# Two feed-forward networks behind pooled attention on one core: attention half-steps re-spaced, low terms moved to VectorE, output products lagging two tiles, weight loads re-queued

## The chip, the core and the metric

The kernel runs on one core of a Trainium2 chip. The metric is the device time of one execution in microseconds. Engines are named as in the profile: PE (TensorE matmuls) and PEld (its weight loads), DVE (VectorE), ACT (ScalarE), POOL (GpSimd), SP (SyncE, which only issues transfers here). Transfers are issued by SP (hardware queue q1) or by POOL (software queue q0).

## The reference, cut to what matters

```python
# attention: q, k, v are (8, 8, 576, 64); k and v are averaged over groups of 8 keys -> 72 keys
scores = (q @ k_p.T) / 8;  attn = exp(scores - max);  attn /= attn.sum() + 1e-9
x = (attn @ v_p) as (4608, 512)
# first network, d_ff = 2048
h = x @ w_in;  x = (s * relu(h)**2 + b) @ w_out
# second network, d_ff = 1536
out = (sigmoid(x @ w_gate) * (x @ w_val)) @ w_out2
```

Weights come as float64. Every large product is made of three float32r products, hi·lo + hi·hi + lo·hi, so each operand is split in a high part (an ACT copy) and a low part (a subtraction).

## The kernel before, in words

**Stage 1 (attention and first network).** The 4608 tokens are 9 blocks of 512. For each block `j` and each of `M1` = 16 slices `m` of d_ff there is one step `i`: `emit_h(i)` (L201, 12 matmuls into `hps`), ReLU, square, scale and bias, `split_g(i)` (L223, makes `gh` on ACT and `gl` on DVE), and `emit_x(i - 2)` (L233, 12 matmuls into four `acc` tiles). Weight slices arrive on SP (`load_wi`, L119) into three buffers. The second network's weights are prepared meanwhile by `prep_w2` (L170): float64 words come in by SP, ACT and DVE convert them (`convert`, L73, `cv` and `raw` tiles), POOL subtracts, SP stores them to DRAM (`w7d`, `wo2d`).

Attention is cut in 18 units of 256 tokens with two halves `t` of 128. A table of positions, two per step (L460 to L487), says where each part of a unit stands; position 2i is ahead of `emit_h(i)`, 2i+1 ahead of `emit_x(i - 2)`. The parts are `scores` (L371: matmuls into `sps`, maximum and subtraction on DVE, exponential on ACT), `norm` (L393: sum and reciprocal on DVE, then POOL makes `pl`, the probabilities of the last 8 keys, and `pm`, those of the first 64), `left` (L408: high copies of `pl` on ACT, low terms on POOL at L414, into `lt`), `turn` (L417: PE transposes `pm` into `tm` and `lt` into `tl`; ACT and DVE copy them out as `t`), and `values` (L439: matmuls into `pv`, split into `xh` and `xl`, which `emit_h` of the next block reads). `sps`, `tm`, `tl` and `pv` share the two buffers of the pool `ps_c`. The pooled keys and values of the next batch are summed on POOL (`kv`, `kbd`, `s` tiles).

From step 16 on PE's order is the program's own (L609). Before that, and on all other engines throughout, a scheduler sets each engine's order from its own model of the times; each engine then works its list strictly in order.

**Stage 2 (second network).** Four pairs of token blocks (`pairs`, L556) are multiplied with seven products in place of eight, then one plain block. In a pair, for each of `M2` = 12 slices: `first_half` (L680, 24 matmuls), `second_half` (L695, 18 matmuls), and `emit_o(p, m, 0)` (L705, 12 matmuls) for the first block of the pair. The gated values of the second block are kept in SBUF, and after the 12 slices come 12 `emit_o(p, m, 1)`: the **kept stretch**. `fetch_w7` (L644) loads 1792 KB for a slice into one of two buffers, from SP. `fetch_wo` (L651) loads 512 KB of `w_out2` into one of three buffers, from POOL. `gen_x` (L568) makes the next pair's operands in the kept stretch from `load`s (L562, POOL, into the six `cv` buffers, which the output copies `eo` use too). The buffers of stage 2 lie where stage 1's weights were, and a load waits for the last reader of the tile it replaces.

```python
for m in range(M2):                    # L739
    fetch_wo((p, 0, m))
    half = first_half(p, m)
    if m:
        emit_o(p, m - 1, 0)
    second_half(p, m, *half)
    fetch_w7(p, m + 2)
emit_o(p, M2 - 1, 0)
```

Of the kernel before, what the change touches and what calls it, by code (L numbers as in the profile page):

```python
# [8 lines left out]
F32 = mybir.dt.float32  # L9
# [3 lines left out]
ALU = mybir.AluOpType  # L13
# [6 lines left out]
def pooled_attention_two_ffn(ctx, tc, q, k, v, v_left, w_in, w_out, s_in, b_in, w_gate, w_val, w_out2, out):  # L20
# [8 lines left out]
    nc = tc.nc  # L29
# [8 lines left out]
    M2 = w_gate.shape[0]  # L38
# [20 lines left out]
    NBLK = len(blocks)  # L59
    w1d = [dram.tile([128, 2, 512], F32, name=f"w1d{m}") for m in range(M1)]  # L60
    w7d = [dram.tile([128, 2, 8 * 256], F32, name=f"w7d{m}") for m in range(M2)]
    wo2d = [dram.tile([128, 2, 512], F32, name=f"wo2d{m}") for m in range(M2)]
    x2d = [dram.tile([128, KD, n], F32, name=f"x2d{j}") for j, (_, n) in enumerate(blocks)]
# [169 lines left out]
    def emit_x(i):  # L233
        j, m = steps[i]
        n = blocks[j][1]
        if m == 0:
            acc[j] = [ps_a.tile([128, 512], F32, tag="a", name="acc")[:, :n] for _ in range(KD)]
        gh, gl = g_t.pop(i)
        hi, lo = wo[m]
        for d in range(KD):  # L240
            f = slice(d * 128, (d + 1) * 128)
            nc.tensor.matmul(out=acc[j][d], lhsT=hi[:, f], rhs=gl, start=m == 0, stop=False)  # L242
            nc.tensor.matmul(out=acc[j][d], lhsT=hi[:, f], rhs=gh, start=False, stop=False)  # L243
            nc.tensor.matmul(out=acc[j][d], lhsT=lo[:, f], rhs=gh, start=False, stop=m == M1 - 1)  # L244
        if m == M1 - 1:
            for d, a in enumerate(acc.pop(j)):
                eo = cvp.tile([128, 512], F32, tag="cv", name="eo")[:, :n]
                if d % 2:
                    nc.vector.tensor_copy(out=eo, in_=a)
                else:  # L250
                    nc.scalar.activation(out=eo, in_=a, func=ACTF.Copy)
                nc.sync.dma_start(out=x2d[j][:, d, :], in_=eo)


    mask = const.tile([128, 3], F32, name="mask")
# [152 lines left out]
    def left(u, t):  # L408
        pm, pl = e_t[u, t]
        lt = at2.tile([128, H, 4, 8], F32R, tag="lt", name="lt")  # L410
        for sl in (0, 2):
            nc.scalar.activation(out=lt[:, :, sl], in_=pl, func=ACTF.Copy)
        for sl in (1, 3):
            nc.gpsimd.tensor_tensor(out=lt[:, :, sl], in0=pl, in1=lt[:, :, sl - 1].bitcast(F32), op=ALU.subtract)  # L414
        e_t[u, t] = pm, lt

    def turn(u, t, part):  # L417
# [44 lines left out]
    def at(pos, fn, *args):  # L462
        events.setdefault(pos, []).append((fn, args))

    for b in range(1, B):
        p = 16 * (b * S // UNIT - 2)
# [9 lines left out]
    for u in range(2, NU):  # L476
        p = 16 * (u - 2) + (2 if u == 2 else 0)
        for t, o in ((0, 0), (1, 4)):
            at(p + o, scores, u, t, 0)
            at(p + o, scores, u, t, 1)  # L480
            at(p + o + 2, norm, u, t)
            at(p + o + 3, left, u, t)
            at(p + o + 6, turn, u, t, 0)
            at(p + o + 6, turn, u, t, 1)
        at(p + 7, load_q, u + 2)
        at(p + 14, values, u, 0)
        at(p + 14, values, u, 1)  # L487

    def probs(u, t):
        scores(u, t, 0, True)  # L490
# [6 lines left out]
    with tc.manual_schedule():  # L497
# [24 lines left out]
        norm(0, 0, True)  # L522
        pool_v_pe(0, "v")
        left(0, 0)
        probs(1, 0)
        norm(0, 1, True)
# [18 lines left out]
    if True:  # L545
# [61 lines left out]
        for i in range(NS):  # L607
            if i == M1:
                pe_order.enter_context(tc.manual_schedule(engines={mybir.EngineType.PE}))  # L609
            store_later()  # L610
            for fn, args in events.pop(2 * i, []):
                fn(*args)
            load_wi(i + 3)
            emit_h(i)
            x, r = divmod(i - 18, 9)
            if i >= 18 and x < M2:
                prep_w2(x, r)
            split_wi(i + 2)
            split_g(i)
            split_wo(i + 1)  # L620
            load_wo(i + 2)
            for fn, args in events.pop(2 * i + 1, []):
                fn(*args)
            if i >= LAG:
                emit_x(i - LAG)
            last = i - (NS - M1)
            if last == 0:
                assert not any(p < 2 * NS for p in events), events
                at_stack.close()
                xop = ctx.enter_context(tc.tile_pool(name="xop", bufs=1, side="right", reuse_waits="tile"))  # L630
            if last in (3, 7):
                gen_x(0, last // 7)


        for i in range(NS - LAG, NS):
            emit_x(i)
        w1_stack.close()
        w7p = ctx.enter_context(tc.tile_pool(name="w7p", bufs=2, reuse_waits="tile"))
        wo2p = ctx.enter_context(tc.tile_pool(name="wo2p", bufs=3, reuse_waits="tile"))
        g2p = ctx.enter_context(tc.tile_pool(name="g2p", bufs=1, reuse_waits="tile"))  # L640
        wk = ctx.enter_context(tc.tile_pool(name="wk", bufs=10, reuse_waits="tile"))
        w7, wo2, g2 = {}, {}, {}

        def fetch_w7(p, m):  # L644
            p, m = p + m // M2, m % M2
            if p < len(pairs):
                a, n = (0, 5) if p == NPAIR else (1, 7)
                w7[p, m] = w7p.tile([128, 2, 7, 2, 128], F32R, tag="w7", name="w7")[:, :, :n]
                nc.sync.dma_start(out=w7[p, m].rearrange("p a b c d -> p a (b c d)").bitcast(F32), in_=w7d[m][:, :, 256 * a:256 * (a + n)])

        def fetch_wo(key):  # L651
            wo2[key] = wo2p.tile([128, 2, 512], F32R, tag="wo2", name="wo2")
            nc.gpsimd.dma_start(out=wo2[key].bitcast(F32), in_=wo2d[key[2]])  # L653

        def product(ps, p, m, x, first, right=None):
            w, r, n = w7[p, m], xo[p][x if right is None else right], pairs[p][1]
# [23 lines left out]
        def first_half(p, m):  # L680
            n = pairs[p][1]
            b0, b1 = (ps_b.tile([128, 512], F32, tag="b", name="pb")[:, :n] for _ in range(2))
            b2, b3 = (ps_c.tile([128, 512], F32, tag="c", name="pc")[:, :n] for _ in range(2))
            product(b0, p, m, 0, True)
            p1 = wk.tile([128, 512], F32, tag="wk", name="wk")[:, :n]
            nc.scalar.activation(out=p1, in_=b0, func=ACTF.Copy)
            product(b1, p, m, 4, True)
            u2 = add2(b1, p1, n)
            product(b2, p, m, 5, True)
            u3 = add2(b2, u2, n)  # L690
            product(b3, p, m, 2, True)
            c22 = add2(b3, u3, n)
            return b0, b2, b3, u2, c22

        def second_half(p, m, b0, b2, b3, u2, c22):  # L695
            n = pairs[p][1]
            product(b0, p, m, 1, False)
            product(b2, p, m, 3, False)
            c21 = add2(b2, u2, n)
            gated(p, m, 0, b0, c21)  # L700
            product(b3, p, m, 6, False)
            c12 = add2(b3, u2, n)
            gated(p, m, 1, c12, c22)

        def emit_o(p, m, t):  # L705
            t0, n = pairs[p]
            if m == 0:
                acc[p, t] = [ps_a.tile([128, 512], F32, tag="a", name="acc") for _ in range(n // 128)]
            gh, gl = g2.pop((p, m, t))
            w = wo2.pop((p, t, m))  # L710
            hi, lo = w[:, 0], w[:, 1]
            for x, a in enumerate(acc[p, t]):
                f = slice(128 * x, 128 * x + 128)
                nc.tensor.matmul(out=a, lhsT=gl[:, f], rhs=hi, start=m == 0, stop=False)  # L714
                nc.tensor.matmul(out=a, lhsT=gh[:, f], rhs=hi, start=False, stop=False)  # L715
                nc.tensor.matmul(out=a, lhsT=gh[:, f], rhs=lo, start=False, stop=m == M2 - 1)  # L716
                if m == M2 - 1:
                    eo = cvp.tile([128, 512], F32, tag="cv", name="eo")
                    if x % 2:
                        nc.vector.tensor_copy(out=eo, in_=a)  # L720
                    else:
                        nc.scalar.activation(out=eo, in_=a, func=ACTF.Copy)
                    r0 = t0 + t * n + 128 * x
                    nc.sync.dma_start(out=out[r0:r0 + 128, :], in_=eo)
# [11 lines left out]
        fetch_w7(0, 0)  # L736
        fetch_w7(0, 1)
        for p in range(NPAIR):
            for m in range(M2):  # L739
                fetch_wo((p, 0, m))  # L740
                half = first_half(p, m)
                if m:
                    emit_o(p, m - 1, 0)
                second_half(p, m, *half)
                fetch_w7(p, m + 2)
            emit_o(p, M2 - 1, 0)
            for m in range(3):
                fetch_wo((p, 1, m))
            gen_x(p + 1, 0)
            gen_x(p + 1, 1)  # L750
            for m in range(M2):
                emit_o(p, m, 1)
                if m + 3 < M2:
                    fetch_wo((p, 1, m + 3))
        if NB % 2:
            for m in range(M2):
                fetch_wo((NPAIR, 0, m))
# [47 lines left out]
```

## Time and profile before

| | |
|---|---|
| median of 3 runs | 1847.71 us (1847.41 to 1849.23) |
| the profiled execution's own time | 1847.31 us |
| its span, first to last instruction | 1845.5 us |
| PE busy | 1752.0 us (95%), 8032 matmuls |
| PEld, DVE, ACT, POOL busy | 1449.9, 933.5, 696.5, 454.2 us |
| mean granted clock of PE | 0.98 of full speed |
| transfers | 364 MB, mean 197 GB/s |

A matmul of 128x512 is drawn about 0.39 us long, while the next one starts 0.23 us after it: matmuls are pipelined. So PE's idle time as the profile gives it (until the next start, from the drawn end) is about 0.16 us short of what a stall costs. "PEclk" is the clock that PE was granted, 1.0 for 2.4 GHz and 0.5 for 1.2 GHz.

### The profile page before, as it was taken

The numbers are of one execution on the slowest core, as the hardware profiler recorded it, in microseconds if no ns is written. First come the engines' busy times: TensorE is split into PE (matmuls) and PEld (weight loads), VectorE is DVE, ScalarE is ACT, GpSimd is POOL, SyncE is SP. The second block draws the span as 40 slices with busy tenths as digits, with TensorE's granted clock in tenths as the row PEclk, the third lists the DMA queues.
The fourth block names the chain that finished last, engine by engine and source line by source line (L and its number), as shares of the span: only waits on it lengthen the run. The fifth ranks groups of instructions, "written<-read, shape, count | busy, mean of one in ns | idle before, by whom it ended". The sixth has DMA issues, their size and how long they took to land.

```text
span 1845.5 us, 21515 instructions
## 1 busy us (share of the span) xinstructions
PE 1752.0 (95%) x8032; PEld 1449.9 (79%) x8032; DVE 933.5 (51%) x1455; ACT 696.5 (38%) x1222; POOL 454.2 (25%) x571
## 2 busy tenths in 40 slices
PE   5888898998999999999998999999999999999999
PEld 4677787887888878788886887788778877887787
DVE  7997745655355555544442445445544554454111
ACT  2666544454454545454442222222222222222111
POOL 6855615425154433322000000200020002000100
PEclk7899999999999999999999999999999999999999
DMA  6775745746375655534433556655575557555764
GB/s 235 267 237 200 262 137 190 251 151 221 99 248 184 224 187 187 201 131 154 139 128 130 197 194 204 242 201 197 192 255 201 196 193 251 194 200 174 248 227 166
DMA packets 103353, 364.22 MB, mean 197 GB/s; under 512 B 10193, under 2 KB 17361, under 8 KB 103249
## 3 DMA queue, kind: packets, MB, share of 16 engines
q1 hardware_dynamic: 84816, 296.78, 46.6%
q0 software_dynamic: 18432, 66.07, 10.6%
q8 instruction: 64, 1.05, 0.2%
q14 instruction: 41, 0.33, 0.1%
HBM read 304.09 MB, written 58.72 MB: 197 GB/s over the span
## 4 chain that ended last, share of the span: by engine, by line
PE 48%; issue 28%; DMA 6%; POOL 5%; DVE 2%; ACT 0%; POOLq 0%; SPq 0%; DVEq 0%; ACTq 0%
PE hps L211 5%; PE hps L213 5%; PE hps L212 5%; PE acc L244 5%; PE acc L242 5%; PE acc L243 5%; PE acc L714 2%; PE acc L716 2%; PE acc L715 2%; DMA wo<-wo2d 2%; PE pc L658 2%; PE pc L660 2%; PE pc L659 2%; DMA raw<-in 2%; PE pb L658 1%
## 5 line engine op out<-in xcount | busy, mean ns | idle before, releaser
L664 DVE TENSOR_TENSOR wk<-pc,wk 128x512 f32<-128x512 f32 x192 | 132.4, 690 | 251.6 <-PE pc L660 251.6
L653 POOL DMA_DIRECT2D wo<-wo2d x108 | 57.1, 529 | 817.6 <-PE acc L716 760.9
L211 PE MATMUL hps<-xl,wi 128*128 128x512 f32 (+1 forms) x584 | 237.6, 407 | 10.6 <-ACT wi L55 6.5
L56 DVE TENSOR_TENSOR gl<-g,gh 128x512 fp32r<-128x512 f32 x204 | 159.6, 782 | 166.4 <-ACT gh L55 161.5
L213 PE MATMUL hps<-xh,wi 128*128 128x512 f32 (+1 forms) x584 | 230.7, 395 | 0.8 <-POOL wi L56 0.8
L212 PE MATMUL hps<-xh,wi 128*128 128x512 f32 (+1 forms) x584 | 229.7, 393 | 0.0
L242 PE MATMUL acc<-gl,woh 128*128 128x512 f32 x576 | 225.8, 392 | 3.9 <-DVE gl L56 3.8
L243 PE MATMUL acc<-gh,woh 128*128 128x512 f32 x576 | 224.5, 390 | 0.0
L244 PE MATMUL acc<-gh,wol 128*128 128x512 f32 x576 | 224.3, 390 | 0.0
L55 ACT ACTIVATE gh<-g 128x512 fp32r<-128x512 f32 x204 | 128.3, 629 | 144.1 <-DVE g L676 141.2
L219 DVE TENSOR_TENSOR g<-g 128x512 f32<-128x512 f32 x128 | 100.2, 783 | 158.5 <-ACT g L215 158.4
L675 ACT ACTIVATE g<-pb 128x512 f32<-128x512 f32 x60 | 35.8, 597 | 359.8 <-PE pb L660 359.8
L659 PE MATMUL pc<-xo,w 128*128 128x512 f32 x432 | 168.1, 389 | 0.0
L658 PE MATMUL pc<-xo,w 128*128 128x512 f32 x432 | 168.1, 389 | 0.0
L660 PE MATMUL pc<-xo,w 128*128 128x512 f32 x432 | 168.1, 389 | 0.0
L220 ACT ACTIVATE g<-g,b_sb,s_sb 128x512 f32<-128x512 f32 x144 | 117.2, 814 | 104.3 <-DVE g L219 103.2
L215 ACT ACTIVATE g<-hps 128x512 f32<-128x512 f32 x144 | 85.2, 592 | 153.0 <-PE hps L213 152.2
L658 PE MATMUL pb<-xo,w 128*128 128x512 f32 x336 | 131.6, 392 | 8.3 <-DMA w<-w7d 8.3
L211 PEld LDWEIGHTS hps<-xl,wi 128*128 128x128 f32 x584 | 112.8, 193 | 33.1 <-ACT wi L55 7.7
L213 PEld LDWEIGHTS hps<-xh,wi 128*128 128x128 f32 x584 | 112.5, 193 | 24.8 <-POOL wi L56 1.0
L659 PE MATMUL pb<-xo,w 128*128 128x512 f32 x336 | 131.2, 391 | 0.0
L660 PE MATMUL pb<-xo,w 128*128 128x512 f32 x336 | 131.2, 390 | 0.0
(109 smaller groups left out, 3342.9 us busy)
## 6 DMA issues: line engine op xcount, KB each, us to landing
w<-w7d SPq DMA_DIRECT2D x48, 1792.0 KB, 7.7
wi<-w1d SPq DMA_DIRECT2D x128, 512.0 KB, 3.7
wo<-wo2d POOLq DMA_DIRECT2D x108, 512.0 KB, 3.8
raw<-in SPq DMA_DIRECT2D x68, 512.0 KB, 4.8
w7d<-raw SPq DMA_DIRECT2D x36, 512.0 KB, 3.7
w<-w7d SPq DMA_DIRECT2D x12, 1280.0 KB, 6.5
kv<-in SPq DMA_DIRECT2D x24, 512.0 KB, 5.4
kv<-in SPq DMA_DIRECT2D x16, 576.0 KB, 4.1
```

The lines of the kernel that those rows point to most:

```text
L55: nc.scalar.activation(out=hi, in_=src, func=ACTF.Copy)
L56: eng.tensor_tensor(out=lo, in0=src, in1=hi.bitcast(F32), op=ALU.subtract)
L211: nc.tensor.matmul(out=ps[:, f], lhsT=hi[:, kk], rhs=c[:, kk, f], start=kk == 0, stop=False)
L212: nc.tensor.matmul(out=ps[:, f], lhsT=hi[:, kk], rhs=a[:, kk, f], start=False, stop=False)
L213: nc.tensor.matmul(out=ps[:, f], lhsT=lo[:, kk], rhs=a[:, kk, f], start=False, stop=kk == KD - 1)
L242: nc.tensor.matmul(out=acc[j][d], lhsT=hi[:, f], rhs=gl, start=m == 0, stop=False)
L243: nc.tensor.matmul(out=acc[j][d], lhsT=hi[:, f], rhs=gh, start=False, stop=False)
L244: nc.tensor.matmul(out=acc[j][d], lhsT=lo[:, f], rhs=gh, start=False, stop=m == M1 - 1)
L658: nc.tensor.matmul(out=ps, lhsT=w[:, 0, x, kk], rhs=r[:, 1, kk, :n], start=first and kk == 0, stop=False, skip_group_check=True)
L659: nc.tensor.matmul(out=ps, lhsT=w[:, 0, x, kk], rhs=r[:, 0, kk, :n], start=False, stop=False, skip_group_check=True)
L660: nc.tensor.matmul(out=ps, lhsT=w[:, 1, x, kk], rhs=r[:, 0, kk, :n], start=False, stop=kk == 1, skip_group_check=True)
L664: nc.vector.tensor_tensor(out=o, in0=ps, in1=b_, op=ALU.add)
```

## The change

- `values(u, 0)` and `values(u, 1)` stand at positions p + 12 and p + 13 in place of both at p + 14. The positions of `turn` are written in another way and stay the same numbers (p + 6 and p + 10).
- `left`'s low terms are computed by DVE, not POOL.
- The four stores of the last block (`x2d` of block 8) are issued by POOL, not SP.
- `fetch_wo` is issued by SP, not POOL, and has four buffers, not three.
- `emit_o(p, m, 0)` comes two slices late, not one; the last two come together after the last `second_half`.
- Of the kept stretch's twelve `w_out2` tiles two are asked for in the last slice and two among the last output products; the fetch of the next pair's second `w7` tile is written after `emit_o(p, 4, 1)`.

```diff
@@ emit_x
-                nc.sync.dma_start(out=x2d[j][:, d, :], in_=eo)
+                (nc.gpsimd if j == NBLK - 1 else nc.sync).dma_start(out=x2d[j][:, d, :], in_=eo)
@@ left
         for sl in (1, 3):
-            nc.gpsimd.tensor_tensor(out=lt[:, :, sl], in0=pl, in1=lt[:, :, sl - 1].bitcast(F32), op=ALU.subtract)
+            nc.vector.tensor_tensor(out=lt[:, :, sl], in0=pl, in1=lt[:, :, sl - 1].bitcast(F32), op=ALU.subtract)
@@ the table of positions
-            at(p + o + 6, turn, u, t, 0)
-            at(p + o + 6, turn, u, t, 1)
+            if t == 0:
+                at(p + 6, turn, u, 0, 0)
+                at(p + 6, turn, u, 0, 1)
+        at(p + 10, turn, u, 1, 0)
+        at(p + 10, turn, u, 1, 1)
         at(p + 7, load_q, u + 2)
-        at(p + 14, values, u, 0)
-        at(p + 14, values, u, 1)
+        at(p + 12, values, u, 0)
+        at(p + 13, values, u, 1)
@@ stage 2
-        wo2p = ctx.enter_context(tc.tile_pool(name="wo2p", bufs=3, reuse_waits="tile"))
+        wo2p = ctx.enter_context(tc.tile_pool(name="wo2p", bufs=4, reuse_waits="tile"))
@@ fetch_wo
-            nc.gpsimd.dma_start(out=wo2[key].bitcast(F32), in_=wo2d[key[2]])
+            nc.sync.dma_start(out=wo2[key].bitcast(F32), in_=wo2d[key[2]])
@@ the loop over pairs
+            kept = [(p, 1, m) for m in range(M2)]
             for m in range(M2):
                 fetch_wo((p, 0, m))
                 half = first_half(p, m)
-                if m:
-                    emit_o(p, m - 1, 0)
+                if m >= 2:
+                    emit_o(p, m - 2, 0)
+                if m == M2 - 1:
+                    fetch_wo(kept.pop(0))
+                    fetch_wo(kept.pop(0))
                 second_half(p, m, *half)
-                fetch_w7(p, m + 2)
-            emit_o(p, M2 - 1, 0)
-            for m in range(3):
-                fetch_wo((p, 1, m))
+                if m < M2 - 1:
+                    fetch_w7(p, m + 2)
+            for m in (M2 - 2, M2 - 1):
+                emit_o(p, m, 0)
+                fetch_wo(kept.pop(0))
             gen_x(p + 1, 0)
             gen_x(p + 1, 1)
             for m in range(M2):
                 emit_o(p, m, 1)
-                if m + 3 < M2:
-                    fetch_wo((p, 1, m + 3))
+                if kept:
+                    fetch_wo(kept.pop(0))
+                if m == 4:
+                    fetch_w7(p, M2 + 1)
```

SP's list where stage 1 ends, before (`wi` is stage 1's weights, `x2d_126` the last block's result, `w` a slice of `w7d`):

```order
L127 DMA wi<-w1d_93 128x1024
L252 DMA x2d_126<-eo 128x512 x2
L649 DMA w_8633<-w7d_94 128x2x1792
L252 DMA x2d_126<-eo 128x512 x2
L649 DMA w_8635<-w7d_95 128x2x1792
L649 DMA w_8711<-w7d_96 128x2x1792
```

and now:

```order
L127 DMA wi<-w1d_93 128x1024
L652 DMA w_8633<-w7d_94 128x2x1792
L652 DMA w_8635<-w7d_95 128x2x1792
L656 DMA wo_8637<-wo2d_106 128x1024
L656 DMA wo_8713<-wo2d_107 128x1024
L656 DMA wo_8789<-wo2d_108 128x1024
L656 DMA wo_8881<-wo2d_109 128x1024
L652 DMA w_8711<-w7d_96 128x2x1792
```

The first two `w` loads no longer stand behind stores of the last block, which are on POOL's list now.

SP's list now where the first pair's last slice ends and its kept stretch begins (`w7d_105` is that slice's weights, `w7d_94` and `w7d_95` the next pair's first two; `wo` from `wo2d_106` on are the kept tiles):

```order
L652 DMA w_9495<-w7d_105 128x2x1792
L656 DMA wo_9635<-wo2d_106 128x1024
L652 DMA w_9583<-w7d_94 128x2x1792
L656 DMA wo_9637<-wo2d_107 128x1024
L652 DMA w_9850<-w7d_95 128x2x1792
L656 DMA wo_9687<-wo2d_108 128x1024
L727 DMA out<-eo 128x512 x2
L656 DMA wo_9713<-wo2d_109 128x1024
L727 DMA out<-eo 128x512 x2
L656 DMA wo_9792<-wo2d_110 128x1024
```

Two kept tiles moved ahead of the next pair's second `w` load. That load, which the program writes after the fifth kept product, stands ahead of the third kept tile all the same.

DVE's list where the second half of unit 6 is normalised, before (the reciprocal ends `norm`; `gl` and `g` belong to the steps, `t` to `turn`):

```order
L398 RECIPROCAL sm<-sm 128x8
L56 TENSOR_TENSOR gl<-g,gh 128x512
L219 TENSOR_TENSOR g<-g 128x512
L56 TENSOR_TENSOR gl<-g,gh 128x512
L219 TENSOR_TENSOR g<-g 128x512
```

and now:

```order
L398 RECIPROCAL sm<-sm 128x8
L56 TENSOR_TENSOR gl<-g,gh 128x512
L219 TENSOR_TENSOR g<-g 128x512
L56 TENSOR_TENSOR gl<-g,gh 128x512
L414 TENSOR_TENSOR lt<-pl,lt 128x8x8 x2
L219 TENSOR_TENSOR g<-g 128x512
```

The low terms, which stood on POOL behind sums of the next batch, now stand on DVE between two of the steps' operations.

## Rows read from the trace of the kernel before

**Rows 1.** Windows by stage (us; busy of each engine with counts, clock, DMA, GB/s)

```profile
0.00:166.00 166.00, 124.25 (x588) 101.63 (x589) 146.89 (x219) 94.61 (x181) 111.43 (x116) 0.89 0.70 241
```

**Rows 2.** Waits of PE (us in total, times, longest)

```profile
PE tl L436 <- POOL lt L414: 11.7, 4, 4.3
PE acc L714 <- DMA wo<-wo2d: 9.4, 7, 2.8
PE pb L658 <- DMA w<-w7d: 8.3, 1, 8.3
...
PE sps L378 <- DVE xl L56: 7.3, 4, 3.7
...
PE acc L714 <- DVE gl L56: 6.4, 4, 1.6
```

**Rows 3.** Timeline of SP and POOL where stage 2's first loads are issued

```profile
957.11 11.20 SPq L127 DMA_DIRECT2D wi<-w1d  x3
...
992.20 0.58 SPq L649 DMA_DIRECT2D w<-w7d  x1
992.83 1.09 SPq L252 DMA_DIRECT2D x2d<-eo  x2
993.96 0.57 SPq L649 DMA_DIRECT2D w<-w7d  x1
...
954.66 0.53 POOL L653 DMA_DIRECT2D wo<-wo2d  x1 [29.83 <-PE acc L244]
```

**Rows 4.** Landing times by tile: `x2d` of 992.8 to 993.6, `w` of 992 to 995

```profile
DMA to landing us min/median/max: 9.7/9.8/9.8
...
DMA to landing us min/median/max: 8.4/11.4/14.4
```

**Rows 5.** Timeline of PE: the end of the first pair's last slice

```profile
1146.02 0.39 PE L659 MATMUL pc<-xo,w 128*128 128x512 f32 x1
1146.25 0.39 PE L660 MATMUL pc<-xo,w 128*128 128x512 f32 x1
...
1148.25 0.50 PE L714 MATMUL acc<-wo,gl 128*128 128x512 f32 x1 [1.61 <-DVE gl L56]
```

**Rows 6.** Windows behind stalls (PE busy third, clock third from last)

```profile
226.00:236.00 10.00, 6.29 (x19) 5.03 (x19) 7.60 (x12) 3.20 (x6) 3.60 (x4) 0.51 0.86 282
318.20:321.20 3.00, 3.00 (x9) 2.42 (x9) 0.40 (x1) 1.95 (x4) 2.26 (x4) 0.51 0.77 225
425.00:430.40 5.40, 5.40 (x15) 4.25 (x14) 0.40 (x1) 1.32 (x3) 5.09 (x8) 0.50 0.72 218
1000.70:1003.80 3.10, 3.10 (x7) 2.47 (x8) 0.00 (x0) 0.14 (x1) 0.00 (x0) 0.50 1.05 398
1160.80:1164.20 3.40, 3.40 (x10) 2.62 (x9) 1.99 (x3) 0.96 (x2) 0.57 (x2) 0.51 0.78 296
```

**Rows 7.** Transfers (page, part 6: count, KB each, median us from issue to landing)

```profile
w<-w7d SPq DMA_DIRECT2D x48, 1792.0 KB, 7.7
```

**Rows 8.** Timeline of POOL, ACT and PE around unit 6's second half

```profile
317.29 0.59 POOL L414 TENSOR_TENSOR lt<-pl,lt 128x64 fp32r<-128x64 f32 x2
...
311.91 0.40 ACT L412 ACTIVATE lt<-pl 128x64 fp32r<-128x64 f32 x2 [0.90 <-POOL pl L405]
...
317.93 0.69 PE L436 MATMUL tl<-ident,lt 128*128 128x128 f32 x2 [4.34 <-POOL lt L414]
```

**Rows 9.** Timeline of DVE: beside a busy POOL, and idle

```profile
303.52 1.61 DVE L56 TENSOR_TENSOR gl<-g,gh 128x512 fp32r<-128x512 f32 x1
...
312.83 1.35 DVE L219 TENSOR_TENSOR g<-g 128x512 f32<-128x512 f32 x1 [3.60 <-ACT g L215]
...
213.26 0.43 DVE L81 TENSOR_SCALAR raw<-raw 128x512 int32<-128x512 int32 x1 [4.37 <-DMA raw<-in]
```

**Rows 10.** Timeline of PE and DVE: the longest way from `turn` to `t`

```profile
524.83 0.60 PE L430 MATMUL tm<-ident,pm 128*128 128x128 f32 x4
...
529.68 0.69 DVE L56 TENSOR_TENSOR t<-tm,t 128x512 fp32r<-128x512 f32 x1
```

## The prediction

> **What bounds the kernel now.** PE does. I read the windows by stage first, then PE's own waits, then the timelines at each long wait, then the clock behind them. In the opening 166 us PE is busy 124 and DVE 147 us [rows 1]: DVE leads there. After it PE is nearly always busy, and what can be won is the short list of stalls in PE's waits [rows 2]. The change aims at five of its entries. Each stall costs about 0.16 us more than its idle time, because a matmul is drawn 0.39 us long while the next starts 0.23 us later [rows 5]. Behind some stalls the clock stands at half, 1.2 GHz in place of 2.4 [rows 6]; of PE's busy time at half clock, half is lost.
>
> **Start of stage 2: -10.0 us.** PE waits 8.3 us for the first `w` load [rows 2]. SP issues it only at 992.2, behind two stores of the last block, although the last `wi` loads are out by 968 (957.1 + 11.2) [rows 3]. In SP's new list the stores are gone and `w` follows `wi`. Its buffer lies where early slices of the first network's output weights were: a `w_out2` load, placed above it, had its buffer free at 954.7 [rows 3]. So `w` can go out at about 968 and, at 7.7 us [rows 7], land at 976, before PE's last product of stage 1 at 992. The stall of 8.3 + 0.16 goes, and with it half of 3.1 us at half clock [rows 6]: 8.5 + 1.5 = 10.0. The stores on POOL cost nothing: their readers come in the plain block, 700 us on. If the buffer were free only with the last product, nothing would be won.
>
> **Output products two slices late: -7.1 us.** After a pair's last slice PE waits 1.61 us for `gl` (1148.25, the slice's last matmul having started at 1146.25) [rows 5], once in each of four pairs, 6.4 in all [rows 2]. Now `emit_o` of slice 10 stands in between: 12 matmuls by 0.23 = 2.7 us, more than the 2.0 us from the end of the slice until `gl` is there. 4 x (1.61 + 0.16) = 7.1. What is hidden costs again if DVE is more than 0.7 us later. Slice 1 runs without output products now, as slice 0 does already without a stall.
>
> **The kept stretch: -13.9 + 2.0 us.** PE waits seven times, 9.4 us, for kept tiles [rows 2]: 9.4 + 7 x 0.16 = 10.5, and two windows of 3.4 us at half clock follow (one shown [rows 6]) at 1.7 each: 13.9. Two tiles are now loaded in the last slice. The third is what is late next: SP's list has it behind the next pair's second `w` load. From the end of the slice, T: `w` is issued at once and lands at T + 7.9. How queued transfers of SP follow each other shows at 994: the last `x2d` store lands at 993.5 + 9.8 = 1003.3, the `w` behind it at 994.0 + 14.4 = 1008.4 [rows 3, 4], 5.1 us for 1792 KB, so 1.46 us per 512 KB. The third tile lands at T + 9.4 and is needed at T + 4 x 2.72 = 10.9. Two output stores (1.5) and the fourth tile (1.5): 12.3, needed 13.6. Two stores and the fifth tile: 15.2, needed 16.3; but two or three loads of `gen_x` (0.73 each) may come between, and it can be 0.4 to 1.1 us late. I take 0.5 per pair, 2.0 in all; between 0 and the whole 13.9. The other kept tiles have three products of lead.
>
> The Trainium skill (DMA: Bandwidth & Descriptors, Queues, rings and completion order) says that the DMA engines take turns between queues and work one queue in its ring's order. By it the move to SP gives up a turn: on POOL's queue the third tile would share the engines with `w` at once, on SP's it stands behind it. By it alone the kept stalls would stay: that is rival K. The trace agrees on the order within SP's queue [rows 4].
>
> **Low terms on DVE and values earlier: -14.0 us.** At 318 and 425 PE waits 4.34 and about as long for `tl`: ACT has both copies at 312.3, but POOL makes the low terms only at 317.3 to 317.9, behind sums for the next batch [rows 8]. DVE idles 3.60 us until 312.83 there [rows 9] and would do two operations (0.3 each, as on POOL [rows 8]) by 313. So 2 x 4.35 = 8.7 goes, and half of 3.0 and of 5.4 us at half clock [rows 6]: 4.2. Earlier `values` free the `ps_c` buffers earlier; of the 7.3 us that `scores` wait for `xl` [rows 2], two short ones (some 1.1 with the 0.16 each) go. The rest is two stalls at 222 to 231. There DVE waits 4.37 us for weights until 213.26 [rows 9] and then has a backlog ahead of `xl`; in its new list the same conversions stand ahead of `xl`, so I let it stay, 0 of up to 9.7 (6.6 idle, half of 6.29 us busy at half clock [rows 6]). `values` now come one step after `turn`: 24 matmuls by 0.227 and the transposes' own 0.6 [rows 10], some 6.0 us. The longest that `t` took after step 16 is 5.5 (524.83 to 530.37) [rows 10]: no new wait.
>
> **The opening: +1.0 us.** Units 0 to 3 put 16 low terms on DVE, 16 x 0.3 = 4.8 us where DVE leads; PE in return loses its `lt` waits there, 11.7 - 8.7 = 3.0 [rows 2]. Net 1.8 if all of DVE's time counts; I take 1.0. The lower end is -3.0. The upper end: beside a busy POOL DVE took 1.61 us for what takes it 0.69 elsewhere, 0.9 more [rows 9, 10]; on all 16 that is 19. The scheduler's order of PE in this part moves too, which no row prices; I put it within the same bounds.
>
> **Sum**, against the profiled execution's own 1847.3 us (0.4 under the median of the runs): 1847.3 - 10.0 - 7.1 - 13.9 + 2.0 - 14.0 + 1.0 = **1805 us**.
>
> **Rivals.**
> K, the kept stretch stays bound by transfers: `w` in front of the third tile keeps the stalls, moved from the POOL queue to SP's. For it: the deferral of `w` is undone in SP's list. Against it: the margins of 1.1 to 1.5 us above. 1805 + 11.9 = 1817.
> O, DVE pays in the opening: the low terms run beside POOL's sums, half of them 0.9 us longer, and nothing of `lt`'s wait comes back: 4.8 + 7.2 = 12.0 in place of 1.0, 1816. The Trainium skill (SBUF — State Buffer, Terms) says that DVE and GpSimd share a port pair as an exclusive lock, held for a whole instruction. By it a low term on DVE waits out a POOL operation, which speaks against this edit; the trace agrees in direction (1.61 against 0.69).
> S, the stall at 222 goes as well, since `values` are in hand earlier than the conversions: 1805 - 9.7 = 1795.
> M, the change of the stores does nothing: `w` waits for its memory, not for SP. 1815. The free buffer at 954.7 speaks against it.
> Q, slower: `wo` loads on SP wait for PE and hold up the `w` loads behind them. A `w` load is issued at a slice's end and needed one slice later, 54 x 0.227 = 12.2 us; it takes 7.7, so 4.5 us late is free, and what is more costs PE that much in each of some 46 slices. At 1 us over, 1805 + 46 = 1851. Against it: the `wo` load in front waits for `emit_o` in the same slice, 18 matmuls or 4.1 us before the `w` buffer comes free.
>
> **How the numbers follow.** Forecast 0.45, K 0.15, O 0.13, S 0.12, M 0.05, Q 0.04, and two of K, O and M together (1826 or so) 0.06. From 1793, just under S, to 1821, over K and O with some error in each, leaves out Q, the pairs and some tails, under 2 in 10. A difference of 0.2%, 3.7 us, is about what a measurement can tell from no change. All but Q are faster by more; Q's milder forms reach no change: 0.94 faster, 0.02 the same, 0.04 slower.
>
> **What would show it.** PE's wait for `w` at the start of stage 2 gone, with the load issued near 968; no wait for `gl` at L714's new line; at most some 2 us of waits for `wo`; no wait of `tl` for `lt` near 313 and 420, and no half clock behind them; PE reaching 166 us's work within a few us of before. It is wrong if kept tiles still stall PE 2 us and more a pair, if `w` is issued after 990, if PE waits for `lt` on DVE, or if a new wait for `w` shows inside the slices.

## The result and the profile after

The changed kernel takes **1814.93 us** (median of 4 runs, 1814.27 to 1816.36), against 1847.56 for the kernel before in runs beside it: a ratio of 0.9824, 95% interval 0.9807 to 0.9841. The forecast was 1805, the range 1793 to 1821. So it is faster by 1.8%, 33 us in place of the 42 that were forecast. The profiled execution took 1814.27 us, its span is 1812.5. Of all the executions below, one (1957.66 us, in e4, at a clock of 0.84 in place of 0.98) belongs to a slower state and is left out.

Where the gain lies is read from the starts of PE's matmuls, one at each border of a stretch (us; the forecast's terms sorted the same way):

| stretch | before | after | difference | forecast |
|---|---|---|---|---|
| up to the first matmul of step 16 | 172.90 | 175.73 | +2.8 | +1.0 |
| from there to stage 1's last matmul | 819.15 | 816.45 | -2.7 | -14.0 |
| from there to stage 2's first | 8.64 | 0.22 | -8.4 | -8.5 |
| stage 2, to the end of the span | 844.9 | 820.1 | -24.8 | -20.5 |

Stage 2 did a little more than was forecast. Stage 1 as a whole gained nothing, where 13 us were forecast. One trace tells a gain of a few us there from none only roughly: the changed kernel and e5 to e8 below have the same list on each engine in stage 1, and their five traces take 804.9 to 811.8 us from the first matmul of step 16 to that of step 143. The opening's row, answering [rows 1] (columns as there):

```profile
0.00:166.00 166.00, 119.50 (x575) 98.03 (x576) 148.65 (x233) 90.70 (x174) 100.91 (x100) 0.89 0.70 240
```

PE's waits in the changed kernel (total, times, longest), answering [rows 2]:

```profile
PE tm L430 <- DVE e L386: 11.4, 4, 4.0
PE acc L242 <- DVE gl L56: 11.0, 6, 5.6
PE sps L378 <- DVE xl L56: 8.3, 4, 3.3
...
PE tl L436 <- DVE lt L414: 5.7, 7, 1.7
```

The waits for `w`, for `wo` and for stage 2's `gl` (8.3, 9.4 and 6.4 us before) are gone: from 985 us to the end the view names no wait at all. At the head now stands a wait of `turn`'s transposes (`tm`) for DVE's `e`, which was 4.6 us before.

**Start of stage 2.** SP's timeline, answering [rows 3], and PE's where stage 1 ends:

```profile
957.24 11.20 SPq L127 DMA_DIRECT2D wi<-w1d  x3
968.49 1.49 SPq L652 DMA_DIRECT2D w<-w7d  x2
970.02 2.94 SPq L656 DMA_DIRECT2D wo<-wo2d  x4
```

```profile
992.18 0.39 PE L244 MATMUL acc<-gh,wol 128*128 128x512 f32 x1
992.40 0.39 PE L661 MATMUL pb<-xo,w 128*128 128x512 f32 x1
```

The first `w` is issued at 968.49, 24 us earlier, and PE goes from one stage to the next without a gap.

**The kept stretch.** PE's last slice of the first pair ends where the output products of slice 10 begin, answering [rows 5], and SP issues around it:

```profile
1133.62 0.39 PE L663 MATMUL pc<-xo,w 128*128 128x512 f32 x1
1133.85 0.39 PE L717 MATMUL acc<-wo,gl 128*128 128x512 f32 x1
```

```profile
1134.04 0.52 SPq L652 DMA_DIRECT2D w<-w7d  x1
1136.76 0.33 SPq L656 DMA_DIRECT2D wo<-wo2d  x1
1138.07 1.11 SPq L727 DMA_DIRECT2D out<-eo  x2
1139.48 0.33 SPq L656 DMA_DIRECT2D wo<-wo2d  x1
```

With T = 1133.85, the third kept tile goes out at T + 2.9 (behind `w`, and when its buffer is free) and, by the transfer view's 6.9 us from issue to landing, is there at T + 9.8; it is needed at T + 10.9. The fourth (7.4 us) is there at T + 13.0 and needed at T + 13.6. Both margins were forecast within 0.7 us, and neither is overdrawn.

**Clock.** In stage 2 there is no stretch at half clock before the last 2 us; before there were three. In stage 1 four are left after step 16, each behind a wait, answering [rows 6] (PE busy third, clock third from last); one of them:

```profile
561.80:565.20 3.40, 3.40 (x9) 2.63 (x9) 2.28 (x6) 2.17 (x7) 3.20 (x5) 0.50 0.96 321
```

**Stage 1.** The wait for `lt` around unit 6's second half, 4.34 us in [rows 8], is down to 0.27, and so is its twin of unit 8. PE and DVE there:

```profile
311.18 0.66 PE L430 MATMUL tm<-ident,pm 128*128 128x128 f32 x4 [0.78 <-POOL pm L405]
312.10 0.41 PE L436 MATMUL tl<-ident,lt 128*128 128x128 f32 x2 [0.27 <-DVE lt L414]
```

```profile
310.44 1.52 DVE L414 TENSOR_TENSOR lt<-pl,lt 128x64 fp32r<-128x64 f32 x2 [2.96 <-ACT lt L412]
```

What took the gain away stands at unit 7, 11 and 13, first halves. PE, DVE and POOL at unit 11:

```profile
556.29 0.39 PE L244 MATMUL acc<-gh,wol 128*128 128x512 f32 x1
560.70 0.63 PE L430 MATMUL tm<-ident,pm 128*128 128x128 f32 x4 [4.02 <-DVE e L386]
```

```profile
555.78 1.99 DVE L414 TENSOR_TENSOR lt<-pl,lt 128x64 fp32r<-128x64 f32 x2 [0.48 <-ACT lt L412]
557.69 1.77 DVE L56 TENSOR_TENSOR gl<-g,gh 128x512 fp32r<-128x512 f32 x1
559.38 0.81 DVE L385 TENSOR_REDUCE mx<-sps 128x4 f32<-128x288 f32 x2
560.11 0.81 DVE L386 TENSOR_TENSOR e<-sps,mx 128x288 f32<-128x288 f32 x2
```

```profile
554.72 0.74 POOL L405 TENSOR_TENSOR pl<-e,sm 128x64 f32<-128x64 f32 x1
...
556.43 3.61 POOL L284 TENSOR_TENSOR kv<-kv 128x512 f32<-128x512 f32 x3
```

`turn(u, 0)` at p + 6 needs the `ps_c` buffers that the second half's `scores` (p + 4) fill, and DVE empties them with `mx` and `e`. In DVE's list those stand behind a step's `gl`, and now `gl` stands behind two low terms. Beside POOL's sums the low terms take 1.99 us and `gl` 1.77; `gl` alone takes 0.69. PE waits 4.02 us and then runs 3.4 us at half clock (561.80, above). The low terms themselves are the smaller part here: ACT has `gh` ready at 557.26, so they hold up `gl` by 0.4 us, and e1 below, without any of them on DVE, still waits 2.80 us at this place. `pl` is late too, behind POOL's sums, and ACT's copies of it stand ahead of the step's own work on ACT.

### The profile page after: what moved, and what is told of

Read it like the earlier page. It is cut to its first block, busy times and chain, and to the rows that moved or that the text cites. A ratio compares the mean times of both kernels' runs of the same rounds, so it can differ in the third digit from the quotient of the medians.

```text
span 1812.5 us, 21425 instructions
## 1 busy us (share of the span) xinstructions
PE 1741.0 (96%) x8032; PEld 1445.5 (80%) x8032; DVE 965.1 (53%) x1527; ACT 693.9 (38%) x1222; POOL 367.1 (20%) x395
## 4 chain that ended last, share of the span: by engine, by line
PE 73%; DVE 9%; DMA 8%; POOL 5%; issue 3%; ACT 2%; SPq 0%; POOLq 0%; DVEq 0%; ACTq 0%
PE acc L719 5%; PE pc L663 5%; PE pc L661 5%; PE acc L717 5%; PE pc L662 5%; PE acc L718 5%; PE hps L211 4%; PE hps L213 4%; PE hps L212 4%; PE acc L242 4%; PE pb L661 4%; PE pb L663 4%; PE pb L662 4%; PE acc L243 4%; PE acc L244 4%; DMA raw<-in 4%
## 5 line engine op out<-in xcount | busy, mean ns | idle before, releaser
L568 POOL DMA_DIRECT2D cv<-x2d x36 | 19.5, 542 | 724.5 <-DMA out<-eo 338.3
L242 PEld LDWEIGHTS acc<-gl,woh 128*128 128x128 f32 x576 | 108.8, 189 | 35.9 <-DVE gl L56 13.9
L661 PE MATMUL pb<-xo,w 128*128 128x512 f32 x336 | 130.7, 389 | 0.0
L662 PE MATMUL pb<-xo,w 128*128 128x512 f32 x336 | 130.7, 389 | 0.0
```

What stands on the lines that cost most here:

```text
L661: nc.tensor.matmul(out=ps, lhsT=w[:, 0, x, kk], rhs=r[:, 1, kk, :n], start=first and kk == 0, stop=False, skip_group_check=True)
L662: nc.tensor.matmul(out=ps, lhsT=w[:, 0, x, kk], rhs=r[:, 0, kk, :n], start=False, stop=False, skip_group_check=True)
```

## The experiments

All times are medians. A stretch between two matmuls is read from one trace of each kernel. The kernel before, run beside each group, took 1846.64 (the first four), 1844.54 (the next four), 1847.84 (three) and 1845.64 us (the last).

### Which edit of stage 1 gave the gain back

Theory V: `values`, one step earlier, put work in front of `e`. Theory D: the low terms on DVE do.

**e1**, low terms back on POOL:

```diff
-            nc.vector.tensor_tensor(out=lt[:, :, sl], ...
+            nc.gpsimd.tensor_tensor(out=lt[:, :, sl], ...
```

> The changed kernel with the low terms back on POOL; values early, stage 2 as changed. Theory D (DVE's list: low terms that wait for POOL's late pl, or run beside POOL, hold up the subtractions of the scores behind them): PE's waits of tm for e fall from 11.4 us back to about the 4.6 of before, with the half clock behind them (some 11 us together), and its waits of tl for lt come back near 313 and 420 (8.7 + 4.2 us): time about 1815 to 1818. Theory V (the early values put the splits of pv ahead of the steps' work on DVE and so make e late): the waits for e stay at 11 us and the tl waits come on top: about 1828.

**e2**, `values` back at p + 14:

```diff
-        at(p + 12, values, u, 0)
-        at(p + 13, values, u, 1)
+        at(p + 14, values, u, 0)
+        at(p + 14, values, u, 1)
```

> The changed kernel with both values back at p + 14; low terms on DVE, stage 2 as changed. Theory D: the waits of tm for e near 355, 560 and 667 stay (11 us in all), scores wait for xl some 1 to 3 us more: 1815 to 1819. Theory V: the waits for e fall to 4.6 us or less with their half clocks: about 1804.

**e3**, both diffs above together, so that only the edits at the end of stage 1 and in stage 2 are left:

> Low terms on POOL and values at p + 14, stage 1 as in the kernel before; only the stores of the last block and stage 2 changed. If the sum by stages of the two traces holds (stage 1 of the changed kernel took what it took before, all of the gain is from the last product of stage 1 on), this is the kernel before less 33 us: 1814.5, the same as the whole change. If stage 1's edits are worth their 14 us and something else ate them, it is about 1828.

**e4**, POOL's `pl` on DVE as well, so that DVE's low terms wait for POOL no longer:

```diff
-            nc.gpsimd.tensor_tensor(out=o, in0=e[:, :, j], ...
+            (nc.vector if o is pl else nc.gpsimd).tensor_tensor(out=o, in0=e[:, :, j], ...
```

> The changed kernel with pl, the probabilities of the last 8 keys, computed by DVE too, so that DVE's low terms no longer wait for POOL (pm stays on POOL). Theory D: the waits of tm for e near 355 and 560 go (7 us, and half of the 3.4 us half clock behind each), the tl waits stay away: about 1804 to 1808. Theory V: nothing changes there, 1815 plus the 36 operations more on DVE, 1815 to 1818.

Measured, with the table's stretches by the first matmuls of steps 16 and 143:

| kernel | median us (ratio to before, 95%) | step 16 at | 16 to 143 |
|---|---|---|---|
| before | | 172.9 | 808.5 |
| changed | 1814.93 (0.9807 to 0.9841) | 175.7 | 805.8 |
| e1 low on POOL | 1811.78 (0.9782 to 0.9822) | 171.9 | 806.0 |
| e2 values at 14 | 1819.02 (0.9839; 0.9818 to 0.9861) | 176.9 | 808.0 |
| e3 both | 1811.88 (0.9782 to 0.9822) | 174.3 | 805.3 |
| e4 `pl` on DVE | 1814.82 (0.9782 to 0.9844) | 177.3 | 804.5 |

The two edits of stage 1 together do not bring the 13 us: e3 without them is at 1811.88, 3 us below the changed kernel, which the intervals do not tell apart. V falls, since e2 keeps the waits for `e` (11.7 us in 4) and is not at V's 1804. D holds for the opening: with low terms on DVE step 16 begins at 174.6 to 177.5 in all nine kernels of this study that have them there, wholly or in first halves (mean 176.3); with low terms on POOL at 170.8 to 174.3 in five (mean 172.4): 3.9 us. Its form "DVE waits for POOL's `pl`" falls with e4: without that wait `tm` still waits 9.7 us for `e` from 166 us on, against 11.4. From step 16 to 143 D is not the whole: in e1, without any low term on DVE, the waits for `e` are 7.8 us (with 2.8 that the view puts down to `kv`, see e10) and those for `lt` are back, and it takes the same 806 us. Early `values` do not settle it either: e1 is 8.2 us ahead of e3 at step 24 (224.5 against 232.8; 2.5 of them were there at step 16), with the wait at 222 down to 1.7 us, and of these 1.7 are left at step 112. The waits of e1 from 166 to 985 us are others than those of the changed kernel:

```profile
PE tl L436 <- POOL lt L414: 8.7, 2, 4.3
PE tm L430 <- DVE e L386: 5.0, 2, 4.0
PE tm L430 <- POOL kv L284: 2.8, 1, 2.8
```

### The edits of stage 2, one undone at a time

Stage 1, which these edits leave alone, differs by up to 7 us between these traces, and the kernel before took 3 us less beside these four than beside the changed kernel. So each is also measured in its profile from the first matmul of step 143 to the end: 831.0 us in the changed kernel, and the same within 0.02 us in the eight others here whose stage 2 is as changed.

**e5**, the last block's stores back on SP:

```diff
-                (nc.gpsimd if j == NBLK - 1 else nc.sync).dma_start(out=x2d[j][:, d, :], in_=eo)
+                nc.sync.dma_start(out=x2d[j][:, d, :], in_=eo)
```

> The changed kernel with one part undone: the last block's four stores are issued by SP again. Theory (SP's list held up the load): the first w load is issued near 983 to 991, behind the first two stores, PE waits some 8 us for it at the start of stage 2 and stands at half clock behind that; +8.5 to +10.0 us, 1823 to 1825. Rival M (the load waits for its memory, and the change's gain there comes from elsewhere): the load goes out at the same time as in the changed kernel, no new wait, 1815 within 2.

1825.18 us, +10.3; from step 143 on +10.8. SP and PE:

```profile
998.95 1.10 SPq L252 DMA_DIRECT2D x2d<-eo  x2
1000.09 0.58 SPq L652 DMA_DIRECT2D w<-w7d  x1
```

```profile
1008.47 0.80 PE L661 MATMUL pb<-xo,w 128*128 128x512 f32 x1 [8.14 <-DMA w<-w7d]
```

`w` waits behind the stores again. The forecast's term of 10.0 is right; rival M falls.

**e6**, output products one slice late:

```diff
-                if m >= 2:
-                    emit_o(p, m - 2, 0)
+                if m:
+                    emit_o(p, m - 1, 0)
...
-            for m in (M2 - 2, M2 - 1):
-                emit_o(p, m, 0)
-                fetch_wo(kept.pop(0))
+            emit_o(p, M2 - 1, 0)
+            fetch_wo(kept.pop(0))
+            fetch_wo(kept.pop(0))
```

> The changed kernel with one part undone: the first block's output products come one slice late, not two. Theory (12 matmuls in between hide gl): PE waits 1.2 to 1.7 us for gl behind the last slice of each of four pairs, +7.1 us, 1822; more, up to 1829, if the clock falls to half behind those waits (1.7 each). Rival (the waits went because the kept tiles came in time, not because of the lag): no wait for gl, 1815 within 2.

1821.02 us, +6.1; from step 143 on +7.7. The wait is back as it was, at 1136.35 behind the slice's last start at 1134.35:

```profile
PE acc L717 <- DVE gl L56: 6.4, 4, 1.6
```

**e7**, `w_out2` tiles issued by POOL, with four buffers:

```diff
-            nc.sync.dma_start(out=wo2[key].bitcast(F32), in_=wo2d[key[2]])
+            nc.gpsimd.dma_start(out=wo2[key].bitcast(F32), in_=wo2d[key[2]])
```

> The changed kernel with one part undone: w_out2 tiles are issued by POOL again, with four buffers and the new order kept. Theory (a fourth buffer and earlier requests carry the gain of the kept stretch, the queue does not): waits for kept tiles below 1.5 us in all, 1815 within 2. Rival K (the queue decides): on POOL's list the tiles stand between stores and loads of gen_x that wait for buffers, and share the DMA engines with the w load; PE waits 4 to 10 us for tiles, with half clock behind some, 1820 to 1829.

1820.94 us, +6.0; from step 143 on +5.1: the time is in K's range, but PE waits only 2.6 us for tiles, three times, between what the theory (1.5) and K (4 to 10) said. POOL's list ahead of one of them:

```profile
1138.80 0.53 POOL L656 DMA_DIRECT2D wo<-wo2d  x1 [6.27 <-PE acc L719]
1141.52 0.53 POOL L656 DMA_DIRECT2D wo<-wo2d  x1 [2.19 <-PE acc L719]
1142.04 1.08 POOL L568 DMA_DIRECT2D cv<-x2d  x2
```

Two loads of `gen_x` go out with the fourth kept tile, which takes 8.4 us to land (7.4 in the changed kernel, where the first of these loads is issued at 1146.3, behind the fifth tile); PE waits for it at 1149.92. The third tile takes 6.9 us here and 6.9 on SP behind `w`: the turn that two queues take, by the Trainium skill (DMA: Bandwidth & Descriptors, Queues, rings and completion order), brought that tile nothing in this case. So the queue did matter; that it did by way of what else it carries fits these rows, but no run separates the two. By the starts of PE's matmuls these waits, and two of under 0.2 us beside them, cost 4.0 of the 5.1 us; another 0.9 stands behind the last matmul (5.2 us to the end of the span, 4.3 in the changed kernel).

**e8**, three buffers for these tiles, on SP:

```diff
-        wo2p = ctx.enter_context(tc.tile_pool(name="wo2p", bufs=4, reuse_waits="tile"))
+        wo2p = ctx.enter_context(tc.tile_pool(name="wo2p", bufs=3, reuse_waits="tile"))
```

> The changed kernel with three buffers for w_out2 tiles, not four; still on SP. Theory (the fourth buffer carries the gain): the second kept tile can be asked for only with the last but one output product, behind the next pair's w load on SP, and lands some 9.4 us after the slice's end where it is needed at 8.1; 1.3 to 1.7 us in each of four pairs, perhaps with half clock behind (1.7 each): 1820 to 1828. Rival (the order on SP's list is enough): 1815 within 2.

1825.74 us, +10.8; from step 143 on +11.4, as the theory had it:

```profile
PE acc L717 <- DMA wo<-wo2d: 6.9, 6, 1.8
```

The fourth buffer carries most of the kept stretch's gain. The program's new order of the fetches has no part in it: with the old order written back, SP's list stays the same but for the tiles' numbers.

### What stands behind the waits of stage 1

**e9**, low terms on DVE only where PE waited for them:

```diff
-            nc.vector.tensor_tensor(out=lt[:, :, sl], ...
+            (nc.vector if t == 1 and u in (6, 8) else nc.gpsimd).tensor_tensor(out=lt[:, :, sl], ...
```

> The changed kernel with the low terms on POOL as before, save in the second halves of units 6 and 8, where they stay on DVE; values at 12 and 13. Theory C (the low terms pay on DVE where POOL is late with them, at t = 1 of units 6 and 8, and cost where they stand in front of gl and the next scores beside a busy POOL, at t = 0 of other units): the two waits of 4.6 us for lt that the kernel with all low terms on POOL shows at 304 and 411 go, with the half clock behind them, the waits for e at 355, 560 of the changed kernel stay away, and 1812 falls by 9 to 13: 1799 to 1803. Rival G (PE that runs ahead meets the prepared weights and gives any gain back): waits of the same size appear at 550 to 670, and the time stays at 1810 to 1815.

**1803.74 us** (0.9765, 0.9746 to 0.9783), 8 under e1, just above C's range. Both waits for `lt` are gone, but of the some 13 us that they and the half clock behind them took in e1, only 6.0 are gained between steps 16 and 143. A wait of 3.09 us for `e` at 348.57, with 3.4 us at half clock behind it, is new against e1, although no low term is on DVE there. POOL, ACT and DVE ahead of it:

```profile
338.79 4.21 POOL L56 TENSOR_TENSOR raw<-cv,raw 128x512 fp32r<-128x512 f32 x3
342.97 0.29 POOL L405 TENSOR_TENSOR pl<-e,sm 128x64 f32<-128x64 f32 x1
```

```profile
343.29 0.41 ACT L412 ACTIVATE lt<-pl 128x64 fp32r<-128x64 f32 x2 [2.07 <-POOL pl L405]
343.60 0.58 ACT L215 ACTIVATE g<-hps 128x512 f32<-128x512 f32 x1
```

```profile
346.63 0.69 DVE L56 TENSOR_TENSOR gl<-g,gh 128x512 fp32r<-128x512 f32 x1 [1.54 <-ACT gh L55]
347.24 0.82 DVE L385 TENSOR_REDUCE mx<-sps 128x4 f32<-128x288 f32 x2
347.97 0.81 DVE L386 TENSOR_TENSOR e<-sps,mx 128x288 f32<-128x288 f32 x2
```

The step's ReLU stands behind ACT's copy of `pl`, that waits for POOL, and POOL is at the second network's weights. From ReLU to `e` follow 5.2 us, so PE waits. C is half right: a low term on DVE is one way to make `e` late, a late `pl` another. Against the changed kernel, e9 gives the price of all low terms on DVE but those two: 11 us (1814.93 and 1803.74), in these traces about half of it ahead of step 16 (175.7 and 170.8) and half behind it.

**e10**, low terms on DVE in first halves only:

```diff
-            nc.vector.tensor_tensor(out=lt[:, :, sl], ...
+            (nc.vector if t == 0 else nc.gpsimd).tensor_tensor(out=lt[:, :, sl], ...
```

> The changed kernel with the low terms of the first halves (t = 0) on DVE and those of the second halves back on POOL. Theory C: it has the worst of both: the waits of 4.6 us for lt near 305 and 412 are back, and the waits of 3 to 4 us for e near 355, 560 and 667 stay; some 9 to 13 above the kernel with all low terms on POOL, 1820 to 1825. Rival G: nothing is tied to a half, the gains and losses cancel, 1812 to 1816.

1814.39 us (0.9809 to 0.9840): a miss for C's number. Both kinds of waits are there as C said (8.7 us for `lt`, 11.3 for `e`), but e1 itself already waits 7.8 us for `e` (2.8 of it stands in the view as `kv`, which the transposes don't read and which ends as the first `e` does), so that only 3.2 us are added between steps 16 and 143, less than two traces of the same lists can differ by.

**e11**, POOL's sums in halves, to tell how DVE and POOL hinder each other:

```diff
-        cuts = -(-n // step)
+        cuts = -(-n // (step // 2 if eng is nc.gpsimd and now[0] >= 24 else step))
...
-            store_later()
+            store_later(); now[0] = i
```

> The changed kernel with the sums of the next batches on POOL cut in pieces of at most 256 elements, not 512, from step 24 on. Theory L (a DVE instruction beside POOL waits for the end of a whole POOL instruction): DVE's gl and g of 128x512, 1.77 us beside POOL now, take 1.2 to 1.4, a low term 0.6 to 0.8 in place of 1.0 to 1.3, and the waits for e near 355, 560 and 667 shrink by 1 us or more each. Theory B (the two share bandwidth, whatever the instruction's length): the durations beside POOL stay at 1.6 to 1.8, and the waits for e stay. The total under L 1805 to 1812, under B 1813 to 1820, since POOL has more instructions.

1809.89 us (0.9780 to 0.9821), which its interval does not tell from the changed kernel. DVE at unit 11:

```profile
554.73 1.22 DVE L219 TENSOR_TENSOR g<-g 128x512 f32<-128x512 f32 x1
557.83 1.44 DVE L414 TENSOR_TENSOR lt<-pl,lt 128x64 fp32r<-128x64 f32 x2 [1.87 <-ACT lt L412]
559.34 1.08 DVE L56 TENSOR_TENSOR gl<-g,gh 128x512 fp32r<-128x512 f32 x1
```

The durations follow L: 1.22 for `g` (1.77 in the changed kernel), 1.08 for `gl` (1.77), 1.44 for two low terms (1.99). The same holds for all of DVE's instructions from 240 to 960 us that run beside these sums and nothing else of POOL's: the longest `g`, `gl` and low term take 1.22, 1.24 and 0.78 us, in the changed kernel 1.78, 1.77 and 1.32. It speaks for an instruction of DVE waiting out one of POOL, as the Trainium skill (SBUF — State Buffer, Terms) has it. The three waits for `e` near 355, 560 and 667 shrank by 0.8 to 1.0 us each, but all waits for `e` still sum to 10.6 us, in 5: POOL's `pl` starts 0.8 us ahead of PE's last matmul before the wait (557.21 and 558.02), in the changed kernel 1.6 (554.72 and 556.29), so that the chain lost in `pl` part of what it gained on DVE.

**e12**, the cure for whatever makes `e` late: e9, and the first half's `turn` half a step later.

```diff
-                at(p + 6, turn, u, 0, 0)
-                at(p + 6, turn, u, 0, 1)
+                at(p + 7, turn, u, 0, 0)
+                at(p + 7, turn, u, 0, 1)
```

> The kernel with low terms on DVE in two places only, and the first half's turn at position p + 7, not p + 6: half a step, 12 matmuls or 2.8 us, later on PE. Theory E (the transposes wait for PSUM buffers that the next half's scores hold until DVE has read them into e, and DVE does so only after the gl of that step, with no slack between p + 4 and p + 6): of the waits of 1.0, 3.2, 2.9, 4.1 and 1.1 us before those transposes some 2 us are left, and the two stretches of 3.4 us at half clock behind them go, 1.7 each: 13 to 14 us below the kernel with the turn at p + 6, 1788 to 1792. Rival G (PE that runs ahead meets the next late operand): the waits move to the copies t, to xl or to gl, and less than 4 us are gained, 1800 to 1806.

**1791.35 us** (1789.35 to 1792.69, five runs; ratio 0.9706, 0.9684 to 0.9727), in theory E's range: 12 us under e9 and 22 to 24 under the changed kernel (by the ratios and by the medians). PE's waits from 166 to 985 us, all of them:

```profile
PE tm L430 <- POOL pm L405: 2.0, 3, 0.7
PE acc L242 <- DVE gl L56: 1.9, 2, 1.2
PE sps L378 <- DVE xl L56: 1.7, 1, 1.7
PE tm L430 <- DVE e L386: 1.4, 1, 1.4
```

From 161.4 us to the last 2 the clock stays at full speed, and steps 16 to 143 take 784.5 us in place of 805.8, far more than two traces of the same lists differ by. The gain comes mainly with the deadline, not with a faster `e`: from the second half's last `scores` matmul to the end of the first `e` it takes 8.1, 7.1 and 10.7 us at units 7, 11 and 13, in e9 8.8, 9.5 and 9.6, while PE reaches p + 6 after 5.8 to 6.8. Position p + 7 with all low terms left on DVE was not run.

## Why the prediction was right, and where it was off

**Start of stage 2 (-10.0): right.** Issue at 968.49 for a forecast 968; undoing it costs 10.3 [e5]. M fell.

**Output products two late (-7.1): right.** The waits of [rows 5] are gone, and undone they return, 7.7 us of stage 2.

**Kept stretch (-13.9 + 2.0): the gain right, the rest too dear.** No wait is left. The 2.0 stood for loads of `gen_x` that come between; the trace has the first at 1146.3, behind the fifth tile. K fell, but e7 shows that the move to SP, which the forecast gave no price, is worth 5 to 6 us with the rest in place, and e8 that the fourth buffer is worth 11; the two do not add up. Of stage 2's last 2 us beyond the terms, 1.3 fit what the sum left out: the first matmul behind a wait is followed after 0.34 us, not 0.23 (1136.35 and 1136.68 in e6): 0.11 for each of 12 waits.

**Low terms and values (-14.0): the step that failed.** Its local claim came true, 4.34 became 0.27. The failed sentence is "no new wait", which was tested for `t` alone. The other operand of `turn`, the PSUM buffers that `e` frees, was already late in the kernel before, in the same view that the forecast used (PE's waits, 166 to 985 us):

```profile
PE tm L430 <- DVE e L386: 4.6, 3, 2.2
```

A chain that is 2.2 us late at times becomes 4 us late once PE arrives earlier or DVE has more to do. Each alone is enough at unit 13: in e1, with no low term on DVE, PE comes to the second half's `scores` 6.5 us earlier than before and `e` only 4.2 us earlier, a wait of 4.03; in e10 PE comes there at the same time as before (658.4 and 658.3) and `e` 3.1 us later, a wait of 3.87. e9 shows it (5 of some 13 us are lost again to a new wait for `e` and its half clock), and e12 that it is this deadline: half a step more and the waits go. What was gained earlier in stage 1, at 222 in e1 or at 318 in the changed kernel, PE lost again at the next first half whose `e` was late.

**The price of a low term** was the second error: "0.3 each, as on POOL". e9 puts the whole of it at 11 us. On DVE its 72 take 0.208, 0.610 and 1.325 us (least, median, most), on POOL before 0.310, 0.323 and 0.870. Here are the two rows (min/median/max in ns):

```profile
L414 DVE TENSOR_TENSOR lt<-pl,lt x72: 208/610/1325, 14.7 to 869.4; 128x64 fp32r<-128x64 f32 x72
```

```profile
L414 POOL TENSOR_TENSOR lt<-pl,lt x72: 310/323/870, 15.7 to 869.4; 128x64 fp32r<-128x64 f32 x72
```

**The opening (+1.0): too cheap**, +2.8 in the profiles, and 3.9 between the two groups of kernels. O was right in kind, a third of it in size. The waits for `lt` that the forecast took off in this part, 3.0 us before, became 5.2 on DVE (5.7 in all, above), one of its own signs of being wrong.

**S**: the stall at 222, two waits of 6.6 us in all and 10 us at half clock before, is one wait of 3.29 us and 3.4 us at half clock in the changed kernel: about half of what S said came. With early `values` and fewer low terms on DVE most of it did: 1.73 us in e1 and 0.48 in e10, with no half clock behind. **Q**: no wait for `w` inside a slice.

The total is 10 us off since the errors, 13 us too much for stage 1 and 4 too little for stage 2, have opposite signs; that is luck. The range was made wide enough for one rival of 10 to 12 us, and by the number alone M (1815), O (1816) or K (1817) would do better than the forecast: only the traces and e5 to e8 show that the terms of stage 2 were right and the one of stage 1 was not.

## What to carry to other kernels

Before a wait is priced as a gain, take the same waiting instruction and list every operand that it needs, with how late each came: PE that arrives earlier waits for the next latest. Give the instruction more distance from its operands before making the operands faster: half a step in a table brought 12 us (e12 against e9), the best change of engine 8 (e9 against e1). And price a small operation by the engine that it moves to, beside the work that runs there, not by the engine that it leaves.

## What the runs showed that was not expected

A DVE operation of 64 elements a partition took six times its shortest, 1.325 against 0.208 us, beside POOL's sums, so that moving it off a slow engine made it slower (0.610 against 0.323 us at the median). And a stretch of program written in another order (the kept tiles' fetches) left SP's list as it was.
